# A two-layer expert chain by seven-product multiplication: sums kept in PSUM, the narrow pair first, operands moved

## The chip, the cores and the metric

The kernel runs on one core of a Trainium2 chip. The metric is device microseconds of one execution, as the median of a few runs. TensorE (PE) multiplies, VectorE (DVE), ScalarE (ACT) and GpSimd (POOL) do the element-wise work, and SyncE (SP) issues all DMAs here, in the order of its queue.

## The reference, cut to what matters

Attention over pooled keys gives x (4608 tokens x 512). Two expert layers follow, and each takes the other's output:

```python
h = x @ w_in                        # 512 -> 2048
g = h * np.cos(h)
x = (g @ w_out).astype(np.float32)  # 2048 -> 512
h = x @ w_in2
g = h * np.clip(h + 3.0, 0.0, 6.0) / 6.0
return (g @ w_out2).astype(np.float32)
```

All products are in fp32 accuracy: each operand is split in a high part (fp32r) and a low part, and hi*hi, hi*lo and lo*hi are summed, so that one product of 128x128 weights with 128x512 columns is three matmuls.

## The kernel before, in words

**First expert.** Attention and the first pass share the first 566 us or so. Weights of w_in and w_out lie as hi and lo in slots of 4096 bytes per partition: `a0` to `a13` (pool_a, feature blocks 0 to 6) and `b0` to `b17` (pool_b, blocks 7 to 15). Tokens go in 9 blocks of 512. A step is one token block with one feature block: 12 matmuls into h (gemm1, L275), the cosine on ACT and DVE (L282 to L304), and two steps later 12 matmuls into the four y banks (gemm2, L318). The first pass takes feature blocks 0 to 4 or 6 of all token blocks and stores partial sums, the second takes the rest. At a block's last step the four y banks are copied out (L325, L328), and L330 adds the first pass's part on POOL.

**Weights of the second expert** are prepared within the second pass. `quads` cuts 16 units into 8 small jobs each (bits, value, sums, split), and `w_ahead` issues one job in each half step behind DVE's L288. The split (L213, L214) copies hi on ACT, takes lo on POOL and stores both to `s_d`.

**Second expert.** Each layer is a 2x2 block product done with seven products. A pair is two column blocks of the same width: `PAIRS` has four pairs of 512 columns and one of 256, the last. In the first phase each of 4 quads `g` of a pair takes seven products `n` of 12 matmuls (`product`, L852). The operand of product n is formed by `operand`: a difference of two blocks where one is needed (L834), hi by ACT (L841), lo by a subtraction (L834). Operands of the next pair are made while g is 3. In the second phase each product n sums over four operands q of its own, made one after the other in a ring of three.

`Quad` says where the seven results go. Four PSUM pools `ps_g` of two banks each; a quad uses two of them (banks of n even and n odd), the next quad the other two. `FRESH` says which product starts its bank anew. Results 0 and 2 are copied to SBUF by ACT (L887), the other five are added by DVE to what lies in SBUF (L892, in the second phase with a scale, L894):

```python
if n == 0:
    self.s1 = copy()
elif n == 1:
    self.out(0, 0, add(self.s1, self.s1))
...
elif n == 5:
    self.out(1, 0, add(self.tile(), self.s2))
else:
    self.out(0, 1, add(self.s2, self.s2))
```

In the first phase `out` is `gate`: Relu on ACT (L956), min and product on DVE (L957), a store to `g_d`. In the second it stores to the output. `load_w` brings one of 28 weights (512 KB) to its place in `SLOTS`, `load_raw` the four y blocks of a pair, `load_g` the four q tiles of one gated block.

**Addresses.** Per partition, pool_a starts at byte 1408 and its slots follow each other every 4096 bytes; tiles of the other pools on the left side also lie at multiples of 128. pool_b and pool_c are laid down from the right end, byte 229344: pool_b's 18 slots start at 155616 + 4096 k, pool_c's two at 147424 and 151520. These are all 96 bytes past a multiple of 128.

The order on each engine comes from the framework's list scheduler, which takes the instructions by their place in the program and by when their inputs are there.

Of the kernel before, what the change touches and what calls it, by code (L numbers as in the profile page):

```python
# [29 lines left out]
def tile_kernel(ctx, tc, q, k, v, wi1, wo1, wi2, wo2, ident_d, mask_d, out):  # L30
# [59 lines left out]
    def big(slot, dtype=F32R):  # L90
        pool = {"a": pool_a, "b": pool_b, "c": pool_c}[slot[0]]
        return pool.tile([P, 1024], dtype, tag=slot, name="w" + slot, bufs=1)
# [19 lines left out]
    def convert_weights(m, fc, half):  # L112
# [8 lines left out]
        a = stg.tile([P, 1024], U32, tag="a", name="a", bufs=2)[:, :HW]  # L121
# [44 lines left out]
    def quads(m, u):  # L166

        wa = stg.tile([P, 1024], U32, tag="a", name="wa", bufs=2)
        wb = stg.tile([P, 1024], F32, tag="a", name="wb", bufs=2)
# [58 lines left out]
        def then_fetch(fn):  # L228
            def run():
                fn()  # L230
                if (m, u) != (1, 7):
                    fetch_quads(*divmod(8 * m + u + 1, 8))
            return run

        return [
            lambda: bits(0), lambda: value(0), lambda: bits(1), then_fetch(lambda: value(1)),
            lambda: sums(0), lambda: sums(1), lambda: split(0), lambda: split(1),
        ]

# [462 lines left out]
    def w_ahead(s, odd):  # L702
        nonlocal quad_at
        if not running:
            if converted == len(wjobs):
                if s < SA + LAG or s >= SB:
                    return
                if not quad_ops:
                    if quad_at == 16:
                        return  # L710
                    if quad_at == 0:
                        fetch_quads(0, 0)
                    quad_ops.extend(quads(*divmod(quad_at, 8)))
                    quad_at += 1
                with tc.issue_after(mark[s - 1 + odd].ins):
                    quad_ops.pop(0)()
                return
            w_convert(0)
# [3 lines left out]
    pool_b = pool_c = None  # L722
# [17 lines left out]
    for slot in range(2 * (T + LAG) + 4):  # L740
# [43 lines left out]
        if live:  # L784
# [7 lines left out]
            while live and npieces < goal:  # L792
                try:
# [16 lines left out]
    SPARE = [f"a{n}" for n in range(7, 13)]  # L810
# [10 lines left out]
    def load_raw(pb, pool):  # L821
        t0, w = PAIRS[pb]
        raws = {}
        for h, t in ((0, 0), (0, 1), (1, 1), (1, 0)):
            r = pool.tile([P, 2, w], F32, tag=f"r{h}{t}", name="rx", bufs=1)
# [4 lines left out]

    def operand(n, raws, temp, hi, lo, e1, e3, e4, el):

        b11, b12, b21, b22 = raws[0, 0], raws[0, 1], raws[1, 0], raws[1, 1]
        sub = lambda eng, o, x, y: eng.tensor_tensor(out=o, in0=x, in1=y, op=ALU.subtract)  # L834
        if n == 2:
            raws["t2"] = temp()
            sub(nc.vector, raws["t2"], b22, b11)
        if n == 3:
            sub(e3, b12, b22, b12)
        src = {0: b11, 1: b21, 2: raws.get("t2"), 3: b12, 4: b11, 5: b21, 6: b22}[n]  # L840
        nc.scalar.activation(out=hi, in_=src, func=AF.Copy)  # L841
        sub(el, lo, src, f(hi))
        if n == 1:
            sub(e1, b11, b12, b11)
        if n == 2:
            sub(e4, b21, b21, raws["t2"])
# [14 lines left out]
    FRESH = [True, True, False, True, True, False, False]  # L861
    turn = 0

    class Quad:


        def __init__(self, wide, scale, pool, out):
            nonlocal turn
            self.at = ps_g[2:] if turn % 2 == 0 else ps_g[:2]
            turn += 1  # L870
            self.wide, self.scale, self.pool, self.out = wide, scale, pool, out
            self.bank = {}

        def begin(self, n):
            if FRESH[n]:
                self.bank[n % 2] = self.at[n % 2].tile([P, 2, N], F32, tag="bank", name="bank")
            return self.bank[n % 2]

        def tile(self):
            return self.pool.tile([P, 2, self.wide], F32, tag="s", name="s", bufs=SB2)  # L880

        def end(self, n):
            got = self.bank[n % 2][:, :, : self.wide]

            def copy():
                t = self.tile()
                nc.scalar.activation(out=t, in_=got, func=AF.Copy, scale=self.scale)  # L887
                return t

            def add(o, x):  # L890
                if self.scale == 1.0:
                    nc.vector.tensor_tensor(out=o, in0=got, in1=x, op=ALU.add)  # L892
                else:
                    nc.vector.scalar_tensor_tensor(  # L894
                        out=o, in0=got, scalar=self.scale, in1=x, op0=ALU.mult, op1=ALU.add
                    )
                return o

            if n == 0:
                self.s1 = copy()  # L900
# [173 lines left out]
```

## Time and profile before

| | us |
|---|---|
| median of 3 runs (1829.96 to 1831.09) | 1830.16 |
| the profiled execution's own time | 1830.89 |
| its span | 1829.1 |
| PE busy in the span | 1701.9 |
| DVE busy in the span | 1261.7 |

The profiled execution's time is 0.73 us above the median, and 1.8 us of it lie outside the span. A busy PE is one with a matmul in flight; matmuls overlap, so the pace of a stream is read from start to start. The granted clock (PEclk) is the share of TensorE's 2.4 GHz that it was given.

### The profile page before, as it was taken

How to read it: one execution, taken by the hardware profiler on the slowest of the kernel's cores; microseconds unless marked ns; L12 is line 12 of the kernel's file. 1: busy time of each engine (PE TensorE's matmuls, PEld its weight loads, DVE VectorE, ACT ScalarE, POOL GpSimd, SP SyncE). 2: the span in 40 equal slices, each digit the busy share in tenths (PEclk: the TensorE clock that was granted, in tenths of full speed). 3: DMA queues.
4: the chain of work that ended last, by engine and by line, in shares of the span. 5: the costliest groups of instructions: out<-in, count | busy, mean ns of one | idle time of the engine just before them, and what ended most of it. 6: DMA issues, size and time to landing. Idle time of an engine off the chain costs nothing. (4 is left out here: it accounts for less than half of the span.)

```text
span 1829.1 us, 21793 instructions
## 1 busy us (share of the span) xinstructions
PE 1701.9 (93%) x7856; PEld 1376.8 (75%) x7856; DVE 1261.7 (69%) x1591; ACT 974.1 (53%) x1471; POOL 494.2 (27%) x329
## 2 busy tenths in 40 slices
PE   4689999999999999999999998989899789999998
PEld 3467778788888877777778786878789568778788
DVE  6998656655777777777774567575756567585856
ACT  3588788887666555556555434343434333333333
POOL 2755543322331333333331213030301021110201
PEclk8799999999999999999999999999999899999999
DMA  7656452223333655566643553232326943425131
GB/s 194 190 176 205 128 157 82 84 76 120 108 122 98 202 201 188 190 205 190 194 156 110 206 201 134 108 138 104 115 116 249 365 148 112 160 82 184 53 109 35
DMA packets 174859, 274.13 MB, mean 150 GB/s; under 512 B 48672, under 2 KB 95904, under 8 KB 174752
## 3 DMA queue, kind: packets, MB, share of 16 engines
q1 hardware_dynamic: 174752, 272.75, 45.1%
q8 instruction: 62, 1.02, 0.2%
q14 instruction: 45, 0.37, 0.1%
HBM read 167.84 MB, written 104.86 MB: 149 GB/s over the span
## 5 line engine op out<-in xcount | busy, mean ns | idle before, releaser
L852 PE MATMUL bank<-wa,wb 128*128 128x512 f32 (+1 forms) x1560 | 344.8, 381 | 19.3 <-DVE wa L834 14.2
L852 PEld LDWEIGHTS bank<-wa,wb 128*128 128x128 f32 x1560 | 277.9, 192 | 83.0 <-DVE wa L834 18.1
L288 DVE SCALAR_TENSOR_TENSOR g<-g,t 128x512 f32<-128x512 f32 x144 | 131.5, 913 | 142.2 <-ACT g L287 141.5
L318 PE MATMUL y<-gh,wb 128*128 128x512 f32 x648 | 219.9, 399 | 9.5 <-ACT ys L328 5.7
L275 PE MATMUL h<-xh,wb 128*128 128x512 f32 x648 | 217.5, 397 | 0.0
L834 DVE TENSOR_TENSOR wa<-gx,wa 128x1024 fp32r<-128x1024 f32 (+1 forms) x120 | 141.1, 1178 | 104.5 <-ACT wa L841 104.0
L841 ACT ACTIVATE wa<-gx 128x1024 fp32r<-128x1024 f32 (+1 forms) x120 | 116.7, 974 | 161.9 <-PE bank L852 139.6
L956 ACT ACTIVATE r<-s,bias_c 128x1024 f32<-128x1024 f32 (+1 forms) x80 | 85.3, 1067 | 186.8 <-DVE s L892 179.4
L275 PE MATMUL h<-xh,wa 128*128 128x512 f32 x504 | 175.7, 405 | 0.0
L852 PE MATMUL bank<-wa,wa 128*128 128x512 f32 (+1 forms) x720 | 157.8, 378 | 17.7 <-ACT wa L841 11.8
L318 PE MATMUL y<-gh,wa 128*128 128x512 f32 x504 | 170.2, 398 | 0.0
L892 DVE TENSOR_TENSOR s<-bank,s 128x1024 f32<-128x1024 f32 (+1 forms) x100 | 111.4, 1115 | 82.1 <-PE bank L852 80.9
L852 PEld LDWEIGHTS bank<-wa,wa 128*128 128x128 f32 x720 | 128.9, 193 | 44.8 <-ACT wa L841 12.0
L318 PEld LDWEIGHTS y<-gh,wb 128*128 128x128 f32 x648 | 122.1, 188 | 44.8 <-ACT ys L328 8.2
L834 POOL TENSOR_TENSOR gx<-gx,t 128x1024 f32<-128x1024 f32 (+1 forms) x20 | 55.3, 2763 | 360.5 <-DVE wa L834 225.1
L275 PEld LDWEIGHTS h<-xh,wb 128*128 128x128 f32 x648 | 122.1, 188 | 29.6
L298 ACT ACTIVATE gh<-g 128x512 fp32r<-128x512 f32 x144 | 90.7, 630 | 97.1 <-DVE g L295 96.9
L291 ACT ACTIVATE g<-g 128x512 f32<-128x512 f32 x144 | 91.0, 632 | 90.1 <-DVE g L288 89.8
L253 POOL TENSOR_TENSOR xl<-xr,xh 128x512 fp32r<-128x512 f32 x72 | 102.0, 1426 | 116.4 <-ACT xh L252 115.7
L318 PE MATMUL y<-gl,wb 128*128 128x512 f32 x324 | 129.0, 398 | 2.2 <-DVE gl L304 2.2
L852 PE MATMUL bank<-xo,wb 128*128 128x512 f32 (+1 forms) x600 | 129.4, 374 | 0.9 <-ACT s L887 0.9
L275 PE MATMUL h<-xl,wb 128*128 128x512 f32 x324 | 128.7, 397 | 0.4 <-POOL xl L253 0.4
(152 smaller groups left out, 3217.5 us busy)
## 6 DMA issues: line engine op xcount, KB each, us to landing
g_d<-r SPq DMA_DIRECT2D x64, 512.0 KB, 2.6
gx<-g_d SPq DMA_DIRECT2D x64, 512.0 KB, 4.2
xr<-x_d SPq DMA_DIRECT2D x72, 256.0 KB, 3.3
wb<-s_d SPq DMA_DIRECT2D x36, 512.0 KB, 7.1
s_d<-wa SPq DMA_DIRECT2D x32, 512.0 KB, 3.5
s_d<-wa SPq DMA_DIRECT2D x32, 384.0 KB, 3.1
yp_d<-ys SPq DMA_DIRECT2D x36, 256.0 KB, 2.3
yv<-yp_d SPq DMA_DIRECT2D x36, 256.0 KB, 3.8
```

The lines of the kernel that those rows point to most:

```text
L253: nc.gpsimd.tensor_tensor(out=xl, in0=t, in1=f(xh), op=ALU.subtract)
L275: nc.tensor.matmul(h, a[:, cs], z, start=(n == 0), stop=(n == 3 * NC - 1))
L288: mark[s] = nc.vector.scalar_tensor_tensor(out=g, in0=g, scalar=MAGIC, in1=t, op0=ALU.subtract, op1=ALU.subtract)
L291: nc.scalar.activation(out=g, in_=g, func=AF.Sin, scale=-TWO_PI)
L298: nc.scalar.activation(out=gh, in_=g, func=AF.Copy)
L318: nc.tensor.matmul(y[c], a, z, start=(first and n == 0), stop=(last and n == 2))
L834: sub = lambda eng, o, x, y: eng.tensor_tensor(out=o, in0=x, in1=y, op=ALU.subtract)
L841: nc.scalar.activation(out=hi, in_=src, func=AF.Copy)
L852: nc.tensor.matmul(bank[:, e, :wide], w[:, j, h, e], z[:, j], start=start and j == 0 and x == 0, stop=stop and j == 1 and x == 2, skip_gro ...
L892: nc.vector.tensor_tensor(out=o, in0=got, in1=x, op=ALU.add)
L956: nc.scalar.activation(out=r, in_=c, func=AF.Relu, bias=bias_c[:, 2:3], scale=1.0)
```

## The change

1. `Quad` takes three of the four PSUM pools, x, z and y. Product 0 starts x, and product 1 starts z. ACT copies x into y (PSUM to PSUM) while product 1 runs, and copies z to SBUF (`half`). Products 2, 4 and 6 add on to x, product 3 to y, product 5 to z. DVE adds twice in a quad: z = x + half after product 2, and c = x + half after product 4. `gate` and `store` read three of four results straight from PSUM. Where a bank was last written narrower than the pair is, two matmuls that nobody reads go before.
2. The second phase scales on ACT: four copies (three where c lies in SBUF already as source and target) by 1/6 in `store`.
3. `operand` uses another form of the seven products: differences are made in place in the raw tiles, with no tile t2. Products 1, 2 and 4 have one ahead of hi, product 3 one behind lo. In the second phase all of them are on DVE; before, one of four was on POOL.
4. `PAIRS` has the 256-column pair first, over token block 0. Its raw tiles and operands are made in the last steps of the first expert (`small_pieces`), with differences and lo parts on POOL. The second phase takes it last.
5. pool_c goes. A pool_u of 4096-byte slots u0 to u22 takes over raw tiles, operands, g tiles and results, in both phases; u20 to u22 hold weights. Ahead of pool_b, on the right side, a tile of 24 floats (96 bytes) is put, so that pool_b's slots start at 155520 + 4096 k.
6. The `quads` of unit u issue the splits of unit u - 1, in 7 jobs instead of 8, and none is issued in the two half steps in which a token block ends. Tag "a" has 4 buffers instead of 2.
7. The weights and g tiles of the second phase are loaded within the last pair of the first phase.

```diff
-    STORED = [0, 1, 4, 5, 3, 2, 6]
-    PAIRS = [(2 * N * n, N) for n in range(NB // 2)] + [(NT - N, N // 2)]
-    SLOTS = [f"a{n}" for n in range(7)] + ["a13"] + [f"b{n}" for n in range(18)] + ["c0", "c1"]
+    STORED = [0, 5, 4, 1, 3, 2, 6]
+    PAIRS = [(0, N // 2)] + [(N + 2 * N * n, N) for n in range(NB // 2)]
+    SLOTS = [f"a{n}" for n in range(7)] + [f"b{n}" for n in range(18)] + ["u20", "u21", "u22"]
...
+    def operand(n, raws, hi, lo, es, el):
+        b11, b12, b21, b22 = raws[0, 0], raws[0, 1], raws[1, 0], raws[1, 1]
+        if n == 1:
+            es.tensor_tensor(out=b12, in0=b22, in1=b12, op=ALU.subtract)
+        if n == 2:
+            es.tensor_tensor(out=b11, in0=b12, in1=b11, op=ALU.add)
+        if n == 4:
+            es.tensor_tensor(out=b11, in0=b22, in1=b11, op=ALU.subtract)
+        src = (b11, b12, b11, b21, b11, b21, b22)[n]
+        nc.scalar.activation(out=hi, in_=src, func=AF.Copy)
+        el.tensor_tensor(out=lo, in0=src, in1=f(hi), op=ALU.subtract)
+        if n == 3:
+            es.tensor_tensor(out=b21, in0=b21, in1=b11, op=ALU.subtract)
...
+                if steps[s - LAG - 1 + odd][5]:
+                    return
...
+                    rest = ctx.enter_context(tc.tile_pool(name="rest", bufs=1, side="right"))
+                    nc.gpsimd.memset(rest.tile([P, 24], F32, tag="rest", name="rest"), 0.0)
                     pool_b = ctx.enter_context(tc.tile_pool(name="pool_b", bufs=1, side="right"))
-                    pool_c = ctx.enter_context(tc.tile_pool(name="pool_c", bufs=1, side="right"))
...
-    FRESH = [True, True, False, True, True, False, False]
+    FRESH = [True, True, False, False, False, False, False]
+    free = [2, 3, 0, 1]
...
+            self.at = free[:3]
+            free[:] = [free[3], free[2], free[1], free[0]]
...
+            if n == 1:
+                self.z = self.bank(1)
...
+                nc.scalar.activation(out=self.cut(self.y), in_=self.cut(self.x), func=AF.Copy)
+                return self.z
+            return {2: self.x, 3: self.y, 4: self.x, 5: self.z, 6: self.x}[n]
...
+            if n == 1:
+                self.half = cols(self.s7(), self.wide)
+                nc.scalar.activation(out=self.half, in_=z, func=AF.Copy)
             elif n == 2:
+                nc.vector.tensor_tensor(out=z, in0=x, in1=self.half, op=ALU.add)
             elif n == 3:
+                self.out(0, 0, y)
             elif n == 4:
+                c = cols(self.c22(), self.wide)
+                nc.vector.tensor_tensor(out=c, in0=x, in1=self.half, op=ALU.add)
+                self.out(1, 1, c)
             elif n == 5:
+                self.out(1, 0, z)
+            elif n == 6:
+                self.out(0, 1, x)
...
-                if more and g == 3:
+                if more and (pb == 0) * 2 + g == 3:
                     make_op(pb + 1, n, raws)
+                if not more and g == 3 and n in (1, 3, 5):
+                    load_g(ORDER2[0], *{1: (1, 1, 1), 3: (0, 1, 2), 5: (1, 0, 3)}[n])
-            if not more and g < 2:
+            if not more:
                 for n in range(7 * g, 7 * g + 7):
                     load_w(1, n)
...
-                operand(n, raws[q], t2, hi, lo, nc.vector, nc.vector, nc.gpsimd, nc.vector)
+                operand(n, raws[q], hi, lo, vec, vec)
```

## Rows read from the trace of the kernel before

**Rows 1.** Page, first part: busy us, share of the span and instructions of each engine.
```profile
PE 1701.9 (93%) x7856; PEld 1376.8 (75%) x7856; DVE 1261.7 (69%) x1591; ACT 974.1 (53%) x1471; POOL 494.2 (27%) x329
```

**Rows 2.** Stretches: length, busy us (instructions) of each engine, PEclk, DMA share, GB/s.
```profile
566.00:1042.25 476.25, 464.18 (x1960) 367.48 (x1960) 327.33 (x468) 270.08 (x445) 138.69 (x82) 1.00 0.55 179
970.00:1042.25 72.25, 72.25 (x310) 58.12 (x309) 30.54 (x43) 35.57 (x58) 7.01 (x5) 1.00 0.47 166
```

**Rows 3.** Stretches of the second expert, its matmuls (L852) alone: length, PE, PEld, PEclk, DMA.
```profile
1042.25:1382.92 340.67, 321.43 (x1344) 258.04 (x1344) 0.97 0.34 128
1382.92:1438.09 55.17, 41.02 (x338) 40.11 (x336) 0.93 0.87 306
1438.09:1782.52 344.43, 326.64 (x1345) 259.81 (x1346) 0.96 0.41 143
1782.52:1825.28 42.76, 40.78 (x337) 39.98 (x335) 1.00 0.09 32
```

**Rows 4.** Timeline of PE: start us, us, line, out<-in, count, [idle before <-releaser].
```profile
1060.57 11.04 PE L852 MATMUL bank<-xo,wa 128*128 128x512 f32 x48
1071.45 4.61 PE L852 MATMUL bank<-wa,wb 128*128 128x512 f32 x19
1075.90 11.41 PE L852 MATMUL bank<-xo,wb 128*128 128x512 f32 x48
1087.15 8.59 PE L852 MATMUL bank<-wa,wb 128*128 128x512 f32 x36
...
1409.26 5.85 PE L852 MATMUL bank<-xo,wb 128*128 128x256 f32 x48
1414.95 4.44 PE L852 MATMUL bank<-wa,wb 128*128 128x256 f32 x36
```

**Rows 5.** Timeline of PE, attention: weights vmh to vrl lie at bytes 136320 to 144511.
```profile
285.35 0.30 PE L567 MATMUL ap_ps<-pth,vmh 128*128 128x320 f32 x1
...
286.08 0.31 PE L567 MATMUL ap_ps<-pth,vmh 128*128 128x320 f32 x1
```

**Rows 6.** Groups of the first expert's matmuls that read pool_b: count, busy us, mean ns.
```profile
L318 PE MATMUL y<-gh,wb 128*128 128x512 f32 x648 | 219.9, 399 | 9.5 <-ACT ys L328 5.7 <-DVE yv L325 2.6 <-ACT gh L298 1.2
L275 PE MATMUL h<-xh,wb 128*128 128x512 f32 x648 | 217.5, 397 | 0.0
L318 PE MATMUL y<-gl,wb 128*128 128x512 f32 x324 | 129.0, 398 | 2.2 <-DVE gl L304 2.2
L275 PE MATMUL h<-xl,wb 128*128 128x512 f32 x324 | 128.7, 397 | 0.4 <-POOL xl L253 0.4
```

**Rows 7.** Waits of PE from 1042.25 to 1438.2: us in total, times, longest.
```profile
PE bank L852 <- DVE s L892: 15.2, 5, 4.6
PE bank L852 <- ACT wa L841: 11.8, 1, 11.8
```

**Rows 8.** Timeline of DVE at the end of a full pair, g = 3.
```profile
1206.61 3.30 DVE L834 TENSOR_TENSOR wa<-t,wa 128x1024 fp32r<-128x1024 f32 x1
1209.83 1.21 DVE L892 TENSOR_TENSOR s<-bank,s 128x1024 f32<-128x1024 f32 x1
```

**Rows 9.** Timeline of PE: a run of 24 matmuls behind a wait.
```profile
1125.65 7.43 PE L852 MATMUL bank<-xo,wc 128*128 128x512 f32 x24 [4.61 <-DVE s L892]
```

**Rows 10.** Groups of element-wise work in the second expert: count, busy us, mean ns, idle before.
```profile
L957 DVE SCALAR_TENSOR_TENSOR r<-r,s 128x1024 f32<-128x1024 f32 x64 | 86.4, 1351 | 33.8 <-ACT r L956 32.5
L956 ACT ACTIVATE r<-s,bias_c 128x1024 f32<-128x1024 f32 x64 | 73.8, 1153 | 164.1 <-DVE s L892 162.1 <-DMA g_d<-r 1.6
L887 ACT ACTIVATE s<-bank 128x1024 f32<-128x1024 f32 x40 | 41.0, 1024 | 35.4 <-PE bank L852 35.2
L834 DVE TENSOR_TENSOR wa<-t,wa 128x1024 fp32r<-128x1024 f32 x16 | 38.2, 2386 | 8.5 <-ACT wa L841 8.5
```

**Rows 11.** Timeline of SP: DMA issues of weights around the end of the first expert.
```profile
1002.96 28.80 SPq L818 DMA_DIRECT2D wb<-s_d  x12
...
1051.38 2.60 SPq L818 DMA_DIRECT2D wb<-s_d  x5
```

More of the change, by code (lines that the diff above doesn't have):

```diff
@@ L90, in big @@
     def big(slot, dtype=F32R):
-        pool = {"a": pool_a, "b": pool_b, "c": pool_c}[slot[0]]
+        pool = {"a": pool_a, "b": pool_b, "u": pool_u}[slot[0]]
         return pool.tile([P, 1024], dtype, tag=slot, name="w" + slot, bufs=1)
@@ L805, in tile_kernel @@
                     w_fetch()
-    STORED = [0, 1, 4, 5, 3, 2, 6]
-    PAIRS = [(2 * N * n, N) for n in range(NB // 2)] + [(NT - N, N // 2)]
-    SLOTS = [f"a{n}" for n in range(7)] + ["a13"] + [f"b{n}" for n in range(18)] + ["c0", "c1"]
-    SPARE = [f"a{n}" for n in range(7, 13)]
+    while small_pieces:
+        small_pieces.pop(0)()
+    lctx.close()
+    pool_u = ctx.enter_context(tc.tile_pool(name="pool_u", bufs=1, reuse_waits="tile"))
+    ps_g = [
+        ctx.enter_context(tc.tile_pool(name=f"ps_g{n}", bufs=1, space=PSUM, reuse_waits="tile"))
+        for n in range(4)
+    ]
     wt = {}
@@ L859, in product @@
                     )
[L861 to L862 removed]
+    FRESH = [True, True, False, False, False, False, False]
+    free = [2, 3, 0, 1]
+    widths = [N] * 4
     class Quad:
[L867 to L880, printed above, removed]
[L882 to L902 removed]
@@ new lines, in __init__, with bank, begin @@
+        def __init__(self, wide, s7, c22, out):
+            self.wide, self.s7, self.c22, self.out = wide, s7, c22, out
+            self.at = free[:3]
+            free[:] = [free[3], free[2], free[1], free[0]]
+        def bank(self, n):
+            return ps_g[self.at[n]].tile([P, 2, N], F32, tag="bank", name="bank")
+        def begin(self, n, w, hi):
+            if n == 0:
+                self.x = self.bank(0)
+                widths[self.at[0]] = self.wide
+                return self.x
+            if n == 1:
+                self.z = self.bank(1)
+                widths[self.at[1]] = self.wide
+                self.y = self.bank(2)
+                if widths[self.at[2]] < self.wide:
+                    for e in range(2):
+                        nc.tensor.matmul(
+                            self.y[:, e], w[:, 0, 0, e], hi[:, 0],
+                            start=True, stop=True, skip_group_check=True,
+                        )
+                    widths[self.at[2]] = self.wide
+                nc.scalar.activation(out=self.cut(self.y), in_=self.cut(self.x), func=AF.Copy)
+                return self.z
+            return {2: self.x, 3: self.y, 4: self.x, 5: self.z, 6: self.x}[n]
@@ L947, in tile_kernel, with load_g @@
+    def load_g(pb, i, t, slot):
+        w = PAIRS[pb][1]
+        home[i, t] = slot
+        for q in range(4):
+            r = big(homes[slot][q], F32)[:, : 2 * w]
+            nc.sync.dma_start(out=r, in_=g_d[pb][i, t, q, :, : 2 * w])
+            gts[pb, i, t, q] = cols(r, w)
+    ORDER2 = [*range(1, len(PAIRS)), 0]
+    for n in range(28):
         load_w(0, n)
```

199 lines of the change are left out of this document (90 added, 109 removed).

## The prediction

> **What bounds the kernel now.** I read the page first: PE is in flight for 93% of the span, and no other engine passes 69% [rows 1]. That leaves two kinds of gain: fewer waits, and a faster pace of the matmuls themselves. So I cut the span in stretches. In the first expert's second pass PE waits for only 12.1 of 476.25 us, at full clock [rows 2]. In the second expert the clock is below 1.00 in three of four stretches, and 1344 matmuls take some 340 us in each phase [rows 3]: 0.254 us apiece, though a stream without waits does better.
>
> How much better shows in the timeline, read from start to start. With weights in pool_a, 48 matmuls take 1071.45 - 1060.57 = 10.88 us, 0.2267 each. With weights in pool_b and the same kind of moving operand they take 1087.15 - 1075.90 = 11.25, 0.2344 each [rows 4]. That is 7.7 ns more, beside 213.3 for 512 columns at 2.4 GHz. With 256 columns pool_b's pace is 5.69 / 48 = 0.1185 [rows 4]; I take 0.120, with a little reserve. What differs between the pools? pool_b sits 96 bytes past a multiple of 128, and also high in the memory. Attention has weights that lie high too, but at multiples of 128: five matmuls of 320 columns take 286.08 - 285.35 = 0.73, 0.146 each [rows 5]. That is 12.7 ns above their 133.3 of columns, where pool_a is 13.4 above its own and pool_b 21.1. So the offset is the likelier cause, not the height. The width differs, so this is an argument and no proof.
>
> The waits of the second expert's first phase are few and large: 15.2 us for DVE's additions, 11.8 once at the start of the second phase [rows 7]. The first kind comes where the next pair's operands are made: POOL's differences and DVE's subtractions run at once, a DVE subtraction of two SBUF tiles takes 3.30 instead of some 1.2, and PE stands behind it; an addition that reads one PSUM tile keeps its 1.21 [rows 8]. Each such wait costs more than itself: the 24 matmuls behind one take 7.43 us, where 24 x 0.2344 and the last one's tail of 0.16 give 5.79 [rows 9]. So a wait of 4.6 costs 6.2.
>
> **The change part by part.** The sum is against the profiled execution's 1830.89 us, 0.73 above the median.
>
> *Offset.* pool_b's slots move to multiples of 128. In the second pass 648 + 648 + 324 + 324 = 1944 matmuls read it [rows 6]; at 7.7 ns each that is 15.0 us, all on the path, since PE is busy for 464 of 476 us and DVE for 327 [rows 2]. The bounds are 0 and 15.0; I take 15.0 by the attention rows. In the second expert the same gain is within the stretches below.
>
> *Splits of the weights.* They leave the half steps in which token blocks end. PE's waits in the second pass are 12.1 us in all, and most are for the copies of y: the groups of gemm2 show 5.7 for ACT's and 2.6 for DVE's in the largest of them [rows 2, 6]. A block of nine steps of 24 x 0.2344 us lasts 50 us, so one block ends in the 72 us from 970 on; the splits are over by then (POOL has 5 instructions there), and PE does not wait at all [rows 2]. I take 7.5 of the 8.3. Seven jobs for eight put more on ACT and DVE in the other steps: bounds -4 (waits of the chain) and 12.1.
>
> *First phase, full pairs.* 1344 x 0.2267 = 304.7 against 340.67 [rows 3, 4]. What remains of the waits? Per quad DVE had five additions of 1.2 and four gate instructions of 1.35 [rows 8, 10], 11.4 of 19 us; now two and four, 7.8. Three gates in four read PSUM, so POOL should not hold them up, as it does not hold the addition in [rows 8]. ACT's copy PSUM to PSUM has no row; the nearest is the copy to SBUF, 1.02 [rows 10], and it has product 1's 12 x 0.2267 = 2.72 us to itself. Up to 1.7 us beyond that row it costs nothing; past it PE waits at product 2. DVE's two additions each have one product as cover as well: 1.2 of 2.72. If DVE is then within a blocked 3.3 us subtraction, PE waits up to 1.8. POOL has two differences and three lo parts per pair, five instructions as before, so such meetings stay possible in the quad that makes operands. I leave 5 us: -31.0. Bounds: nothing left (-36), and the waits as they are now (-7.4, the pace alone: 4 x 240 of the matmuls read pool_b or pool_c, at 7.7 ns each).
>
> *Narrow pair first, and the start of the second phase.* 55.17 us now [rows 3], of which 11.8 are the wait for g tiles [rows 7]. These now come a whole pair earlier, from data stored long before. 336 x 0.120 = 40.3 stay, and I leave 3. The two unread matmuls per bank are 0.5 us. -11.9. Its own cover is tighter: a product lasts 1.44 us, and 28 weights of 512 KB, 14.7 MB, are wanted in 40 us. 12 of them are issued before the first expert ends, and five only at 1051.38, behind y stores [rows 11]. The same order would bring those for products 20 on, needed 29 us after the start: covered. If that cover went, PE would wait for what of 14.7 MB at 306 GB/s [rows 3] (48 us) exceeds 40: 8 us. Making the operands of the narrow pair on POOL and ACT lies under the last steps, where POOL is busy for 7 of 72 us [rows 2]. SP has the loads of y for it in its queue between stores of y; if these are late, the loads of weights behind them are too, which is the same 8 us.
>
> *Second phase.* 304.7 + 40.3 = 345.0 against 344.43 + 42.76 [rows 3]. Now tile t2 is a single buffer: difference, hi and lo of one operand run one after the other, and with POOL at work lo takes 2.39 [rows 10], so 1.2 + 1.0 + 2.39 is more than the 12 x 0.2344 = 2.81 us that PE takes. In place, without POOL, DVE needs two instructions of 1.2 for 2.72 us of PE, for products 1 to 4 in a row: 32 + 2 additions x 1.2 = 41 of 43.5 us. That is tight, and the four scaling copies of 1.02 on ACT [rows 10] lie beside it. I leave 8.5: 353.5, -33.7. Bounds: -42.2, and -7.4 for the pace alone. The tail behind the last matmul stays: an addition goes, a copy comes. All loads of this phase now lie in the first phase's last pair: 28 weights, 16 g tiles and 16 stores of 512 KB, 31.5 MB in 76 us or 414 GB/s, above the 306 of rows 3. But seven weights and twelve tiles (10 MB) are wanted only 10 us or more after its end, and 21.5 MB in 76 us are 283 GB/s: covered, barely. If not, PE waits at most as long as it does at this place today, 11.8 [rows 7].
>
> Sum: 15.0 + 7.5 + 31.0 + 11.9 + 33.7 = 99.1; 1830.89 - 99.1 = 1731.8. I say **1732 us**.
>
> **The rivals.** *The pace stays.* The offset is not the cause. 15.0 and 1920 x 7.7 ns = 14.8 fall out of the sum: 1762. For it: no stretch shows pool_b at another offset, and at 256 columns pool_b is only 11.8 ns above the columns. Against: rows 5. By the Trainium skill's page "SBUF — State Buffer", section "Specifications (TRN2)", SBUF is read in lines of 16 bytes; 96 is a multiple of 16, so by that rule alone the shift changes nothing and 1762 it is. The trace's 7.7 ns say that something beyond it counts.
>
> *Waits come back where operands are made.* In each of the four quads that make the next operands, both of DVE's additions come late by what one came late before: 4 x 2 x 6.2 = 49.6, of which 8 are in the sum: 1773. For it: each result now feeds the next but one product, so a late DVE is felt at once. Against: DVE has fewer instructions there.
>
> *Slower.* The place is the same, the hand-over of x between PE and DVE (products 4 and 6) in all 20 quads of the first phase. A miss of today's size costs 6.2; from 99 / 6.2 = 16 misses on the kernel is slower, less than one per quad. Both missed everywhere: 32 x 6.2 + 8 x 3.1 - 8 = 215 more, 1947. Against: without operand work DVE is idle for 11 of 19 us.
>
> **How the numbers follow.** The forecast has 0.65, its own range 1711 (no wait left at all: 15.0 + 12.1 + 36.0 + 14.9 + 42.2 = 120) to 1748 (twice the 16.5 us of waits that I leave in the second expert). The pace that stays has 0.15, waits that come back 0.14, slower or even 0.06. 1710 to 1778 leaves out the last and the far ends of the others. 0.2% is 3.7 us, about what a measurement can tell. Faster 0.94, within 0.01, slower 0.05.
>
> **What would show it.** The pace of a stream with pool_b weights: 0.2267 or 0.2344. PE's waits for the y copies in the second pass: near 1 us, not 8.3. The three quads at the end of full pairs without a wait of 4 us; the second phase starting within 1 us of the first; the clock at 1.00 in all stretches. I am wrong if PE's waits on DVE or on ACT's copies show in every quad, or if the second phase's stretches stay above 315 us.

## The result and the profile after

The changed kernel takes 1758.77 us (median of 4 runs, 1751.55 to 1761.35) against 1830.25 of the kernel before in the same comparison: a ratio of 0.9602, 95% interval 0.9573 to 0.9631. It is faster by 71.5 us, where 99 were forecast. That lies inside the range, but outside the forecast's own 1711 to 1748. The profiled execution took 1757.72, its span 1755.9. One execution further down (of the run e9_before_split_on_vector) ran at a granted clock of 0.837 and took 1908.01 us; neither its time nor its profile is used there.

The page's first line, which answers to [rows 1]:

```profile
PE 1664.5 (95%) x7858; PEld 1375.2 (78%) x7858; DVE 1162.3 (66%) x1530; ACT 986.1 (56%) x1489; POOL 438.4 (25%) x316
```

The stretches of the changed kernel: the first pass from its first step on, the second pass, the 256-column pair of the first phase, the full pairs of the first phase, the same of the second phase, and its 256-column pair. Columns as in [rows 2].

```profile
75.58:557.47 481.89, 453.79 (x2267) 368.24 (x2267) 334.73 (x560) 358.44 (x630) 192.95 (x163) 0.97 0.40 124
557.47:1047.12 489.65, 474.10 (x2041) 384.45 (x2040) 355.41 (x486) 287.18 (x475) 161.37 (x98) 0.99 0.54 176
1047.12:1101.92 54.80, 46.12 (x338) 45.09 (x337) 24.70 (x29) 21.63 (x31) 14.55 (x8) 0.84 0.59 203
1101.92:1406.90 304.98, 304.98 (x1348) 252.53 (x1347) 143.57 (x120) 125.87 (x119) 35.56 (x15) 1.00 0.49 179
1406.90:1711.50 304.60, 304.60 (x1345) 252.23 (x1344) 219.80 (x190) 140.60 (x136) 0.00 (x0) 1.00 0.43 149
1711.50:1752.00 40.50, 40.50 (x337) 40.31 (x335) 24.82 (x38) 19.68 (x32) 0.00 (x0) 1.00 0.10 34
```

The two passes of the kernel before, cut at the same steps:

```profile
76.19:547.39 471.20, 449.28 (x2267) 364.30 (x2267) 331.52 (x560) 360.62 (x632) 190.53 (x163) 0.99 0.41 127
547.39:1042.25 494.86, 482.79 (x2041) 382.61 (x2040) 340.56 (x487) 283.57 (x469) 144.04 (x87) 1.00 0.55 178
```

With [rows 3] for the second expert this gives the account:

| stretch, us | before | forecast | after |
|---|---|---|---|
| first pass | 471.2 | 471.2 | 481.9 |
| second pass | 494.9 | 472.4 | 489.6 |
| 256-column pair, first phase | 55.2 | 43.3 | 54.8 |
| full pairs, first phase | 340.7 | 309.7 | 305.0 |
| second phase | 387.2 | 353.5 | 345.1 |

The second expert came out nearly as forecast: -78.2 against -76.6. In its full pairs PE is busy for every microsecond, at full clock, and the last three stretches above are the pace and nothing else. The first expert did not: +5.4 against -22.5. That the second expert's total is so close is chance: its full pairs and its last pair gained 13.1 us more than forecast, and the first 256-column pair 11.5 less.

**The pace.** The timeline of PE in a full pair of the changed kernel, weights in pool_b:

```profile
1121.23 13.76 PE L897 MATMUL bank<-wu,wb 128*128 128x512 f32 x60
1134.83 5.38 PE L897 MATMUL bank<-wa,wb 128*128 128x512 f32 x23
```

(1134.83 - 1121.23) / 60 = 0.2267, where [rows 4] had 0.2344.

**The 256-column pair.** Timelines of PE, ACT, POOL and SP (DMA issues) in this pair:

```profile
1057.19 10.24 PE L897 MATMUL bank<-wa,wb 128*128 128x256 f32 x84
1072.68 2.90 PE L897 MATMUL bank<-wa,wb 128*128 128x256 f32 x12 [5.24 <-issue]
1076.26 2.90 PE L897 MATMUL bank<-wa,wb 128*128 128x256 f32 x12 [0.69 <-issue]
1081.92 12.51 PE L897 MATMUL bank<-wa,wb 128*128 128x256 f32 x84 [2.76 <-ACT bank L937]
```
```profile
1062.71 1.06 ACT L752 ACTIVATE wu<-wu 128x1024 fp32r<-128x1024 f32 x1 [1.78 <-DMA wu<-y_d]
1068.48 2.00 ACT L752 ACTIVATE wu<-wu 128x1024 fp32r<-128x1024 f32 x2 [4.71 <-POOL wu L746]
1070.39 0.67 ACT L1008 ACTIVATE wu<-bank,bias_c 128x512 f32<-128x512 f32 x1
```
```profile
1066.08 2.37 POOL L746 TENSOR_TENSOR wu<-wu,wu 128x1024 f32<-128x1024 f32 x1 [17.46 <-DMA wu<-y_d]
```
```profile
1049.56 2.17 SPq L877 DMA_DIRECT2D wb<-s_d  x3
1051.82 1.67 SPq L877 DMA_DIRECT2D wu<-s_d  x3
1053.54 2.94 SPq L889 DMA_DIRECT2D wu<-y_d  x4
1057.51 2.89 SPq L1012 DMA_DIRECT2D g_d<-wu  x3
```

Product 14, the first of the third quad, begins 5.2 us late. Its bank is freed by the first quad's last gate, and that (L1008 at 1070.39) stands on ACT behind three copies hi (L752) for the next pair, one of which waits for POOL's difference and that for a raw load. The gate could not have run much earlier: it writes the tile of the quad's first gate, whose store was issued at 1057.51 and landed 10.4 us later, at 1067.94, where such stores take 2.6 us at the median; the DMA engines are 0.95 busy in the pair's first 20 us. The waits of 8.7 us are not all. Behind them 48 matmuls (12, 12 and the first 24 of the 84) run at half the clock, 5.04 / 24 = 0.21 us each from start to start, where 84 took 1057.19 - 1047.12 = 10.07 before, 0.120 each. The stretches ahead of the first wait, of the 12 matmuls behind it and of the 24 behind the third show the granted clock at 1.00 (2.4 GHz) and near 0.50 (1.2 GHz):

```profile
1047.12:1067.40 20.28, 20.28 (x169) 20.10 (x167) 6.63 (x9) 5.63 (x9) 2.75 (x3) 1.00 0.95 346
1072.68:1075.58 2.90, 2.90 (x12) 2.60 (x12) 2.90 (x2) 0.51 (x1) 1.80 (x1) 0.50 0.63 239
1081.92:1086.96 5.04, 5.04 (x24) 5.04 (x24) 0.88 (x2) 0.00 (x0) 1.31 (x1) 0.51 0.42 123
```

**Block ends of the second pass.** The largest group of gemm2's matmuls, which answers to the first line of [rows 6], has 11.5 us of idle time, against 9.5 before; over the whole pass PE is idle for 15.5 us, against 12.1:

```profile
L324 PE MATMUL y<-gh,wb 128*128 128x512 f32 x648 | 217.9, 397 | 11.5 <-ACT ys L334 6.8 <-DVE yv L331 2.4 <-ACT gh L304 2.1
```

One block end, in the timelines of POOL, DVE, ACT and PE:

```profile
893.39 2.37 POOL L214 TENSOR_TENSOR wa<-wb,wa 128x1024 fp32r<-128x1024 f32 x1 [2.78 <-ACT wa L213]
895.71 1.73 POOL L336 TENSOR_TENSOR ys<-ys,yv 128x512 f32<-128x512 f32 x1
899.22 1.28 POOL L336 TENSOR_TENSOR ys<-ys,yv 128x512 f32<-128x512 f32 x1 [1.78 <-ACT ys L334]
```
```profile
887.62 0.69 DVE L310 TENSOR_TENSOR gl<-g,gh 128x512 fp32r<-128x512 f32 x1
...
893.86 2.45 DVE L310 TENSOR_TENSOR gl<-g,gh 128x512 fp32r<-128x512 f32 x1 [0.50 <-ACT gh L304]
896.23 1.76 DVE L294 SCALAR_TENSOR_TENSOR g<-g,t 128x512 f32<-128x512 f32 x1
897.91 0.68 DVE L331 TENSOR_TENSOR yv<-y,yv 128x512 f32<-128x512 f32 x1
...
899.29 0.68 DVE L331 TENSOR_TENSOR yv<-y,yv 128x512 f32<-128x512 f32 x1
```
```profile
898.02 0.63 ACT L297 ACTIVATE g<-g 128x512 f32<-128x512 f32 x1 [2.56 <-DVE g L294]
898.56 0.58 ACT L334 ACTIVATE ys<-y 128x512 f32<-128x512 f32 x1
```
```profile
898.64 0.50 PE L324 MATMUL y<-gh,wb 128*128 128x512 f32 x1 [1.55 <-DVE yv L331]
```

POOL's lo of a split runs until 895.76 and holds DVE's `gl`, which takes 0.69 us at 887.62, where POOL is silent, and 2.45 here; the next `g` is then held by POOL's addition. DVE's copy of y stands behind both, and PE waits 1.55 us for it. On ACT the next copy of y stands behind L297, which waits 2.56 us for the same `g`.

### The profile page after: what moved, and what is told of

Same layout as the page of the kernel before. It is cut to its first block, busy times and chain, and to the rows that moved or that the text cites. A ratio compares the mean times of both kernels' runs of the same rounds, so it can differ in the third digit from the quotient of the medians.

```text
span 1755.9 us, 21639 instructions
## 1 busy us (share of the span) xinstructions
PE 1664.5 (95%) x7858; PEld 1375.2 (78%) x7858; DVE 1162.3 (66%) x1530; ACT 986.1 (56%) x1489; POOL 438.4 (25%) x316
## 3 DMA queue, kind: packets, MB, share of 16 engines
q8 instruction: 62, 1.02, 0.2%
## 5 line engine op out<-in xcount | busy, mean ns | idle before, releaser
L897 PE MATMUL bank<-wa,wb 128*128 128x512 f32 (+1 forms) x1368 | 293.1, 362 | 8.7 <-issue 5.9
L897 PEld LDWEIGHTS bank<-wa,wb 128*128 128x128 f32 x1368 | 235.8, 194 | 47.2 <-issue 6.4
L324 PE MATMUL y<-gh,wb 128*128 128x512 f32 x648 | 217.9, 397 | 11.5 <-ACT ys L334 6.8
L752 ACT ACTIVATE wa<-wu 128x1024 fp32r<-128x1024 f32 (+1 forms) x130 | 127.3, 980 | 142.7 <-PE bank L897 124.8
L897 PE MATMUL bank<-wu,wb 128*128 128x512 f32 (+1 forms) x792 | 198.4, 386 | 0.0
L897 PEld LDWEIGHTS bank<-wu,wb 128*128 128x128 f32 x792 | 148.8, 188 | 29.9
L297 ACT ACTIVATE g<-g 128x512 f32<-128x512 f32 x144 | 91.0, 632 | 105.9 <-DVE g L294 105.5
L281 PEld LDWEIGHTS h<-xh,wb 128*128 128x128 f32 x648 | 121.9, 188 | 25.4
L310 DVE TENSOR_TENSOR gl<-g,gh 128x512 fp32r<-128x512 f32 x111 | 100.6, 906 | 46.3 <-ACT gh L304 45.5
L753 DVE TENSOR_TENSOR wa<-wu,wa 128x1024 fp32r<-128x1024 f32 (+1 forms) x80 | 89.5, 1123 | 54.4 <-ACT wa L752 54.3
L1008 ACT ACTIVATE wu<-bank,bias_c 128x1024 f32<-128x1024 f32 (+1 forms) x60 | 61.8, 1030 | 99.5 <-PE bank L897 87.7
L897 PE MATMUL bank<-wa,wa 128*128 128x512 f32 (+1 forms) x552 | 117.4, 359 | 0.0
L301 DVE TENSOR_TENSOR g<-h,g 128x512 f32<-128x512 f32 x144 | 98.6, 685 | 27.8 <-ACT g L297 26.9
```

The source lines that it names most:

```text
L281: nc.tensor.matmul(h, a[:, cs], z, start=(n == 0), stop=(n == 3 * NC - 1))
L297: nc.scalar.activation(out=g, in_=g, func=AF.Sin, scale=-TWO_PI)
L301: nc.vector.tensor_tensor(out=g, in0=hs[s], in1=g, op=ALU.mult)
L310: eng.tensor_tensor(out=gl, in0=gs[s][0], in1=f(gh), op=ALU.subtract)
L324: nc.tensor.matmul(y[c], a, z, start=(first and n == 0), stop=(last and n == 2))
L753: el.tensor_tensor(out=lo, in0=src, in1=f(hi), op=ALU.subtract)
```

## The experiments

Each edit is against the changed kernel unless said otherwise; the "three edits" of the last two runs are those of e7_three_edits. Step 60 is the first of the second pass.

**The first pass: two buffers.** The quads' tiles alternate between two tags, so that tag a is back at two buffers.

```diff
-        a = stg.tile([P, 1024], U32, tag="a", name="a", bufs=4)[:, :HW]
+        a = stg.tile([P, 1024], U32, tag="a", name="a", bufs=2)[:, :HW]
...
-        wa = stg.tile([P, 1024], U32, tag="a", name="wa", bufs=4)
+        wa = stg.tile([P, 1024], U32, tag="aq"[: 1 + (u % 2)], name="wa", bufs=2)
```

> The changed kernel, but the weights of the first expert are converted with two buffers as before (quads keep four, under two tags). In the profile of the changed kernel PE reaches step 12 of the first pass 11.1 us later than before, and stays 10 us late up to step 60. Theory (the four buffers let the scheduler put weight conversions of the first pass elsewhere on DVE, ACT, POOL and SP): the 10 us come back, step 60 starts within 1 us of before's 547.4 us, the kernel takes 1749 us. Rival (attention's DMAs or the moved addresses of its tiles cost the 10 us, the buffers nothing): step 60 stays at 557, the kernel at 1758.

1746.39 us, ratio to before 0.9551 (0.9536 to 0.9565). The first pass is back at its old length:

```profile
75.49:546.94 471.45, 448.56 (x2267) 362.49 (x2267) 332.13 (x560) 360.61 (x632) 190.58 (x163) 0.99 0.41 127
546.94:1036.19 489.25, 473.88 (x2042) 383.56 (x2040) 355.43 (x486) 286.98 (x475) 161.37 (x98) 0.99 0.54 177
```

So the four buffers cost about 10 us there. With them some weight conversions stand elsewhere among attention's work: of the lo parts on POOL (L145), one runs at 164.65 in the changed kernel and the like one at 145.11 here, the last one before 235 us at 174.37 there and at 191.31 here. The granted clock between 107 and 235 us is 0.93 in the changed kernel, and 1.00 here up to 224 us, where the same steps end. That this order is what costs the time is likely, but was not traced.

**The offset alone, in the kernel before.**

```diff
+                    rest = ctx.enter_context(tc.tile_pool(name="rest", bufs=1, side="right"))
+                    nc.gpsimd.memset(rest.tile([P, 24], F32, tag="rest", name="rest"), 0.0)
                     pool_b = ctx.enter_context(tc.tile_pool(name="pool_b", bufs=1, side="right"))
```

> The kernel before with one thing added: a tile of 24 floats at the right end, so that the slots of pool_b and pool_c start at multiples of 128. Theory (the offset of 96 bytes costs 7.7 ns per matmul of 512 columns): the pace with pool_b weights goes from 0.2344 to 0.2267 us, 15 us of the second pass of the first expert and 15 us of the second expert fall, as far as PE is the bound there: 1800 to 1812 us. Rival (the pace came from something else that the whole change brought, such as the addresses of the moving operands): 1830 us, pace 0.2344.

1816.79 us, 0.9934 (0.9917 to 0.9951), above the theory's 1800 to 1812. Start to start, the pace of gemm1 with pool_b's weights goes from 0.2344 to 0.2267. Of some 30 us only 12 come through:

```profile
546.78:1038.81 492.03, 475.57 (x2041) 382.28 (x2040) 339.96 (x487) 283.32 (x469) 141.27 (x87) 0.99 0.55 179
```

The second pass gains 2.8 us of the 15.0, and the second expert 9.1. The pace did its part in the second pass: 97 x 0.2267 + 1944 x 0.2344 = 477.7 us became 2041 x 0.2267 = 462.7. What lies above it grew from 17.2 to 29.3. PE's idle time, from 12.1 to 16.5, shows only part of that: a matmul is in flight for 0.39 us, so a wait of less than 0.16 does not count as idle, and in two stretches (729.6 to 733.0 and 941.3 to 944.7) the granted clock is 0.50, where the kernel before had 1.00 throughout.

**The offset undone in the changed kernel**: the tile has 32 floats, so that pool_b again lies 96 bytes past a multiple of 128.

```diff
-                    nc.gpsimd.memset(rest.tile([P, 24], F32, tag="rest", name="rest"), 0.0)
+                    nc.gpsimd.memset(rest.tile([P, 32], F32, tag="rest", name="rest"), 0.0)
```

> The changed kernel with the tile at the right end of 32 floats instead of 24: pool_b's slots are 96 bytes past a multiple of 128 again, all else as changed. Theory: pace 0.2344 with pool_b weights; 1728 such matmuls of 512 columns in the second expert, 13.3 us, and 1944 in the first, of which waits there take some back: 13 to 28 us more, 1772 to 1787 us. Rival (the pace of the changed kernel comes from its operands' addresses alone): 1758 us.

1769.12 us, 0.9676 (0.9658 to 0.9693): 10 us slower, a little less than the 13 to 28 expected, with the pace at 0.2344 again for weights in pool_b, and at 0.2267 still for those in pool_a and pool_u. The second pass takes 490.2 us, 0.5 more than with the shift; 9.3 more lie in the second expert.

**POOL out of the splits.**

```diff
-            nc.gpsimd.tensor_tensor(out=lo, in0=w, in1=f(hi), op=ALU.subtract)
+            nc.vector.tensor_tensor(out=lo, in0=w, in1=f(hi), op=ALU.subtract)
```

> The changed kernel, with the lo parts of the second expert's weights (L214) on DVE instead of POOL. In the second pass PE waits for the copies of y and for gl, and DVE's instructions with two SBUF inputs last up to 2.45 us while POOL has such a lo part. Theory (POOL holds DVE up, DVE's late chain holds ACT's queue up, and the y copies stand in it): without these 32 POOL instructions PE's waits in the second pass fall from some 20 us to under 10, the kernel to about 1748 us, though DVE has some 25 us of work more there. Rival (DVE is simply full there, 5.4 us per step being less than before): no gain or a loss, 1758 to 1768 us.

1736.61 us, 0.9495 (0.948 to 0.9511), 22 less than the changed kernel and 11 better than the theory. The second pass:

```profile
560.87:1029.93 469.06, 465.12 (x2042) 383.70 (x2040) 345.71 (x518) 289.03 (x475) 97.39 (x66) 1.00 0.58 184
```

DVE has 32 instructions more and is busy for 345.7 us instead of 355.4: the held-up ones are short again. PE's idle time falls from 15.5 to 3.9, and none of it is for a copy of y any more.

**Operands of the first full pair one quad later.**

```diff
-                if more and (pb == 0) * 2 + g == 3:
+                if more and (pb == 0) * 1 + g == 3:
```

> The changed kernel (1758.8 us), but the operands of the first full pair are made in the third quad of the 256-column pair instead of the second, 11 us later. Theory: the narrow pair takes 47.5 us instead of 43 because product 1's difference waits on POOL for raw y loads that land after the quad has begun, and ACT's and DVE's later instructions stand behind it; one quad later the loads have landed, the 8 us of waits at 1072 to 1082 shrink to 2 or less, the narrow pair takes 42 to 44 us and the kernel about 1753 (1750 to 1756). Rival: the waits come from DVE's and ACT's own amount of work in a quad of 11 us (seven operands on top of gates and sums); then they move with the operands to the third quad, the pair stays at 47 to 48 us and the time within 1757 to 1761, or gets longer if the operands are not ready by the first full pair.

1752.91 us, 0.9583 (0.9568 to 0.9597). The number is the theory's, the mechanism isn't, and a difference of 6 us is not clear of the changed kernel's own 1751.55 to 1761.35. Product 14 still waits 4.75 us, 25.6 us after the pair's start, and product 16 waits 2.05. The pair is 2.7 us shorter, and 3.4 us come from the first pass, which the edit doesn't touch. The place in the source hardly moved the instructions: ACT still has three of these copies ahead of the second quad's gates.

**The moved splits undone**: eight jobs, splits at their own end, block ends not skipped, two buffers. To be read against the two-buffer kernel.

```diff
-            [lambda: before(0)],
...
-            [lambda: bits(1), lambda: before(1)],
...
+            lambda: sums(0), lambda: sums(1), lambda: split(0), lambda: split(1),
...
-                if steps[s - LAG - 1 + odd][5]:
-                    return
```

> The changed kernel with the seven-job quads undone: eight jobs again, each quad's splits at its own end, block ends not skipped, and two buffers of tag a as before the change; all else as changed. To be read against the changed kernel with two buffers in two alternating tags (1746.4 us). Prediction's own theory: the moved splits gain 7.5 us by freeing the block ends; then this kernel takes about 1754 and its second pass waits about 7 us more. Rival (from the trace of the changed kernel): the move gained nothing, since POOL's lo of a split still holds DVE's instructions up in the half steps before a block ends, whichever half step that is; then this takes 1743 to 1748, and with the splits no longer crowded into other jobs' half steps perhaps a few us less; step 60 lies at 547 in either case.

1756.27 us, 0.9601 (0.9587 to 0.9616), 9.9 more than the two-buffer kernel. So the prediction's step holds, and the rival that I had read from the trace falls. Of the 6.9 us of idle time that the move saves in the second pass (22.3 to 15.4) only 1.8 are waits for the copies of y; 3.6 are waits for `gh`.

```profile
548.33:1046.94 498.61, 476.30 (x2041) 381.61 (x2040) 344.58 (x486) 286.17 (x475) 157.86 (x98) 0.99 0.53 173
```

The second pass of this kernel is also 6.6 us longer than that of the offset alone (492.0), which differs there mainly by the operands of the narrow pair; 6.0 of it lie in the six steps from step 126 on, 43.9 us instead of 37.9. POOL's timeline of the changed kernel shows where they run, among the last unit's two splits (L214) and not under the last steps:

```profile
961.03 1.84 POOL L214 TENSOR_TENSOR wa<-wa,wa 128x768 fp32r<-128x768 f32 x1 [6.74 <-ACT wa L213]
962.90 1.67 POOL L746 TENSOR_TENSOR st<-st 128x512 f32<-128x512 f32 x1
...
965.97 4.33 POOL L753 TENSOR_TENSOR wa<-st,wa 128x512 fp32r<-128x512 f32 x3
...
973.28 2.39 POOL L214 TENSOR_TENSOR wa<-wb,wa 128x1024 fp32r<-128x1024 f32 x1
```

**Three edits at once**: two buffers, splits on DVE, operands one quad later (the diffs above).

> The changed kernel with three edits at once: two buffers in two alternating tags, the splits' lo on DVE, the first full pair's operands one quad later. Theory: the three losses lie in different stretches and add: 1758.8 - 12.4 (first) - 22.2 (second) - 6 (third) = 1718 us, 1714 to 1724. Rival: the first two overlap, because both act on the order in which the weight chain's instructions stand among attention's and the gate chain's, or because the clock falls elsewhere; then 1726 to 1737, no better than the splits on DVE alone.

1725.23 us, 0.943 (0.9416 to 0.9444), just above the theory's 1714 to 1724. The first two add (1758.8 - 12.4 - 22.2 = 1724.2); the third gives nothing.

**POOL back in the second phase.**

```diff
-                operand(n, raws[q], hi, lo, vec, vec)
+                operand(n, raws[q], hi, lo, vec, pool if n > 4 else vec)
```

> The changed kernel, but in the second phase the lo part of the last two of each seven operands goes to POOL again, as before the change (40 instructions of 2.4 us). Theory (the second phase's gain comes from taking POOL out, since its instruction holds DVE's two-operand ones for its whole length): waits of PE come back in the second phase, where there are none now, 10 to 30 us in all: 1769 to 1789. Rival (the gain comes from the sums in PSUM and the operands made in place alone, and POOL beside DVE costs nothing that PE feels, as there are three operand buffers ahead): 1757 to 1763.

The edit does not restore the kernel before, which had one difference of every four on POOL there, 20 instructions, and every lo on DVE; it puts 40 lo parts on POOL.

1766.9 us, 0.9658 (0.9641 to 0.9674), 8 more than the changed kernel: between the two ranges. PE's waits in the second phase, of which there were none, and DVE's differences for product 1 of full pairs, 1221 ns on average before this edit:

```profile
PE bank L897 <- POOL wa L753: 5.5, 3, 2.1
PE bank L897 <- POOL wu L753: 2.0, 1, 2.0
```
```profile
L746 DVE TENSOR_TENSOR wu<-wu,wu 128x1024 f32<-128x1024 f32 x11 | 21.0, 1913 | 29.4 <-DMA wu<-g_d 29.3
```

There are four waits of some 2 us, 7.5 in all, each for POOL's own result. DVE is held up too, but PE never waits for it; the ring of three is the likely cover. So 40 instructions on POOL would cost about 8 us of the second phase's 42. What the 20 differences of the kernel before cost was not measured.

**The splits on DVE in the kernel before**, first by itself, then with the 24 floats.

> The kernel before, with the lo part of the weights' splits on DVE instead of POOL, nothing else. Theory (POOL's split is what makes the waits of the second pass, before the change as after it, because it holds DVE's two-operand instructions for its length): six steps take 33.7 us each time, as they do now where no block ends, instead of up to 38.3; the 78 steps from step 60 on take 13 x 33.7 = 438 instead of 455 us: 1829.8 - 17 = 1813 (1809 to 1818). Rival (the waits come from the copies of y themselves, and four more us of work per quad on DVE, 68% busy, eat up what POOL's absence frees): 1826 to 1834.

> The same, and the 24 floats that move the weights to multiples of 128. Theory (the offset alone gained 13 of a possible 30 us because in the second pass the makers of operands, held up by POOL, set the pace at block ends; freed of that, the whole 15.0 us of the second pass come through, beside the 9 of the second expert): 24 us below the split on DVE alone, 1789 (1785 to 1793), six steps in 32.6 us each. Rival (what kept the gain small is something else, the clock or DVE's load): 13 us below the split on DVE alone, 1797 to 1803.

1815.65 us (the median of three), 0.9928 (0.9905 to 0.995), and 1803.6, 0.9856 (0.9831 to 0.9881). The first theory's time holds (15 us, within its bounds); its steps were not seen. The second falls: the offset adds 12 again, not 24. The second pass with both is

```profile
546.94:1024.92 477.98, 468.70 (x2042) 381.34 (x2040) 352.44 (x519) 283.49 (x469) 74.74 (x55) 1.00 0.57 184
```

PE still waits 9.3 us, most of it at the block ends, where splits stand as before the change. With POOL out and the splits away from the block ends it was 3.9: it takes both until PE nearly sets the pace there.

**Operands in the last quad**, with the three edits.

```diff
-                if more and (pb == 0) * 1 + g == 3:
+                if more and g == 3:
```

> The kernel with the three edits (1725.2 us), but the first full pair's operands are made in the last quad of the 256-column pair, 11 us later still, as in the other pairs. There the third quad still waits 4.7 and 2.1 us, since SP issues the raw loads only at 1024 to 1028, behind the stores of y and the last weights, and POOL's first difference begins at 1036.5. Theory: with the loads landed long before, these waits go and the narrow pair takes 41 to 42 us instead of 44.5: 1722 (1720 to 1724). Rival: seven operands in the 11 us of that quad are too many for POOL's five instructions of 2.4 us, so the first full pair starts waiting for its last operands: 1726 to 1732.

1723.4 us, 0.9424 (0.9406 to 0.9442). That is within the theory's range, but hardly different from 1725.23, and the mechanism is not the theory's: product 14 still waits 4.67 us, 25.7 after the pair's start. The place in the source is not what decides.

**Order on ACT, and the narrow pair's operands on DVE**, with the three edits.

```diff
-        operand(n, small, t[:, 0], t[:, 1], nc.gpsimd, nc.gpsimd)
+        operand(n, small, t[:, 0], t[:, 1], nc.vector, nc.vector)
...
+                    if pb == 0:
+                        with tc.issue_after(relu[7].ins):
+                            make_op(1, n, raws)
```

(`relu[7]` is the second quad's last Relu.)

> The kernel with the three edits (1725.2 us) with two more, whose effects lie in different stretches. First, the instructions that make the first full pair's operands are ordered on ACT behind the second quad's last gate. In all variants so far product 14 of the narrow pair waits 4.7 to 5.6 us at 25 to 26 us after the pair's start, wherever in the source the operands are made, since ACT has hi of products 0 to 2 ahead of the second quad's gates in its order, and the one of product 1 waits for POOL's difference and that for raw loads. Theory: with the gates ahead, product 14 and 16 do not wait, and the 23 products from the pair's start on end after 38 to 40 us instead of 44.9. Rival: product 14 waits for something else (its weight, the store of a gate tile); then 44 to 46 as before. Second, the narrow pair's own operands are made on DVE instead of POOL, where they are also bound to the steps they are meant for; POOL's run of twelve of them falls on the last split now and makes the six steps from step 132 on take 38.4 us. Theory: 32.6 to 34. Rival (DVE's extra 10 us just delay the gate chain): 36 or more. Both right: 1716 us (1713 to 1719); both wrong: 1723 to 1727.

1715.23 us, 0.9373 (0.9357 to 0.9389), the fastest of all. The second pass and the narrow pair:

```profile
545.96:1008.62 462.66, 462.66 (x2042) 382.71 (x2040) 347.94 (x529) 289.51 (x475) 80.26 (x55) 1.00 0.57 187
1008.62:1057.94 49.32, 43.37 (x337) 42.71 (x336) 23.45 (x29) 21.71 (x31) 13.15 (x7) 0.93 0.61 215
```

The second edit did all it should: PE doesn't wait once, and 2041 matmuls x 0.2267 are 462.7. Of the first, the rival holds, so it is chance that the time lies where both were to be right. Timelines of PE, ACT and SP, and the time from issue to landing of the first gate's store:

```profile
1032.83 5.46 PE L897 MATMUL bank<-wa,wb 128*128 128x256 f32 x24 [3.90 <-issue]
```
```profile
1031.32 1.39 ACT L1009 ACTIVATE wu<-bank,bias_c 128x512 f32<-128x512 f32 x2 [8.89 <-DMA g_d<-wu]
```
```profile
1015.05 3.57 SPq L889 DMA_DIRECT2D wu<-y_d  x4
1019.59 14.82 SPq L1013 DMA_DIRECT2D g_d<-wu  x6
```
```profile
DMA to landing us min/median/max: 11.7/11.7/11.7
```

With ACT's queue free the same gate waits 8.9 us for a gate tile: there are three for four gates, and the first one's store is issued only at 1019.59, behind the stores of y, six weights and four raw loads, and takes 11.7 us to land. In the changed kernel that store landed at 1067.94, and ACT's copies were out of the way at 1070.39. So two things end close together there, and taking one away moves product 14 only from 25.4 to 24.2 us after the pair's start. That fewer loads ahead of the stores, or a fourth gate tile, would end the wait wasn't tried.

## Why the prediction came out as it did

**The mechanism of the second expert's full pairs was right.** The expert's sum was -76.6 and measured -78.2. *First phase, full pairs*: 31.0 forecast, 35.7 measured; no wait is left, where I left 5. *Second phase*: 33.7 and 42.1; the 8.5 that I left are not there either. DVE keeps up at 219.8 of 304.6 us: with POOL silent its lo takes 1.22 us and not the 2.39 of [rows 10]. The copy PSUM to PSUM, for which I had no row, takes 1.01, as good as the 1.02 of the nearest row. The groups of DVE and ACT in the second expert of the changed kernel, 128x1024 alone:

```profile
L753 DVE TENSOR_TENSOR wa<-wu,wa 128x1024 fp32r<-128x1024 f32 x65 | 79.1, 1223 | 45.2 <-ACT wa L752 45.2
```
```profile
L937 ACT ACTIVATE bank<-bank 128x1024 f32<-128x1024 f32 x20 | 20.2, 1009 | 21.0 <-PE bank L897 21.0
```

POOL's absence is part of the second phase's gain, as the run shows that put 40 instructions on it; how large a part is open, since the kernel before had others there, and fewer. Nor did any run take the sums in PSUM, the operands in place and the earlier loads apart: the trace shows that the waits of [rows 7] are gone and that the pace is left, not which of the three ended which wait. The offset alone brought 9.1 of the 78.

**Narrow pair first**: 11.9 forecast, 0.4 measured. The wait of 11.8 us did go, but 336 x 0.122 and the unread matmuls are 41.4 of the 54.8 us: 13.4 came in its place, and "the clock at 1.00 in all stretches" failed here, with 0.84. The step that failed is "28 weights of 512 KB, 14.7 MB, are wanted in 40 us ... covered". I counted the weights alone. It was not a weight that was late: SP's queue carries, behind those weights, the raw loads and the stores that free the gate tiles, and these landed 9 to 11 us after their issue. That the price of 8 us that I gave for a lost cover is close to the 8.7 of waits is chance. The lower clock behind them accounts for the rest: 24 x (0.21 - 0.120) = 2.2, and two runs of 12 that take 2.90 each where 12 x 0.120 and a last one's tail of 0.16 give 1.6, 2.6 more.

**The splits**: 7.5 forecast; undoing them, together with the two buffers that they brought, costs 9.9. Right in size. But "PE's waits for the y copies in the second pass: near 1 us, not 8.3" was wrong: they are 6.8 and 2.4 still, since POOL's instruction goes on holding DVE in the half steps just before block ends. The larger part of the gain came from `gh`: 3.6 of 6.9 us.

**The offset** is the cause of the pace; both runs of it show 7.7 ns. By the Trainium skill's page "SBUF — State Buffer", section "Specifications (TRN2)", with lines of 16 bytes alone, the shift would have changed nothing; the measurement decides. The term failed all the same, at the step "15.0 us, all on the path, since PE is busy for 464 of 476 us". In the second pass it brought 2.8 in the kernel before and 0.5 in the changed one. PE's busy share said that PE is nearly always busy, not that it ends every wait: around the block ends the makers of operands and the copies of y end last, and there a faster PE only waits longer.

**The narrow pair's operands** were costed at nothing, "under the last steps, where POOL is busy for 7 of 72 us". They begin some 25 us ahead of those 72, between the last splits, and cost 6.6.

**The first pass** had no term at all. Of item 6 I weighed the jobs and passed over the four buffers of tag a, which the weight conversions of the first pass share: 10 us.

So the second pass adds up:

| second pass, us | length | step |
|---|---|---|
| before | 494.9 | |
| offset alone | 492.0 | -2.8 |
| with the narrow pair's operands (splits not moved) | 498.6 | +6.6 |
| with the splits moved (two buffers) | 489.3 | -9.4 |
| the changed kernel | 489.6 | +0.4 |
| splits' lo on DVE | 469.1 | -20.6 |
| narrow pair's operands on DVE too, two buffers | 462.7 | -6.4 |

The rivals fall. The pace did not stay; its 1762 lies near the result by chance. Waits did not come back in the quads that make the operands of full pairs, nor at the hand-over of x.

What stays open is which instruction's new place costs the first pass its 10.7 us: idle time rose by 6.2 and the matmuls themselves by 4.5, but the one was not traced to the other.

## What to carry to other kernels

A faster pace is worth its count times its gain only in stretches where PE itself ends last; look at what ends the waits there, not at the busy share. When work leaves POOL, count what its instructions held up on DVE, too: here moving 32 instructions to the busier engine made that engine less busy in the stretch and the kernel 22 us faster. And when a buffer count or a queue's order changes, list everyone who shares the tag or the queue: two of the three largest misses here were a tag's other user and a store at the end of SP's queue.

## What the runs showed of the hardware

The start address of the weights sets the pace of 512-column matmuls: 96 bytes past a multiple of 128 they take 0.2344 us each, at a multiple 0.2267, in the kernel before, in the changed one, and in both with the offset exchanged. Offsets other than 0 and 96 were not run.

A DVE instruction with two SBUF inputs stands still while POOL's runs (2.45 us for 0.69), and one that reads PSUM and SBUF does not (0.68 for `yv` at 899.29, with POOL at work from 899.22 on). The Trainium skill's page "SBUF — State Buffer", section "SBUF: two separate sides", states that the pair of ports the two engines share is locked for a whole instruction; the trace agrees.

A wait of 5.2 us in a stream of 256-column matmuls, with two shorter ones (0.7 and 2.8 us) soon behind it, brought 48 of them at half the granted clock, 0.21 us from start to start instead of 0.120: 4.8 us on top of 8.7 of waits.
